# An RWKV-5 attention with a SmeLU feed-forward, rewritten with two tokens per partition and one written order of steps

## The chip, the cores and the metric

One core of one Trainium2 chip. The core has a matrix engine (TensorE, PE), a vector engine (VectorE, DVE), an engine for activation functions (ScalarE, ACT), a general one (GpSimd, POOL), a sequencer for transfers (SyncE, SP) and 16 DMA engines. Each engine works through its own queue in order and waits on semaphores. The metric is device time in microseconds.

## The reference

Four batches, 8 heads, 768 tokens, 48 values per head, all float32. First a linear attention whose state decays by `w` per token and head dimension, with a bonus `u` for the token itself; then two matrix products with a piecewise activation (384 to 2048 to 384).

```python
for t in range(S):
    cur = einsum('bhd,bhe->bhde', u * k[t], v[t])
    y[t] = einsum('bhd,bhde->bhe', r[t], state + cur)
    state = w * state + einsum('bhd,bhe->bhde', k[t], v[t])
x = y as (B * S, H * D)                      # 3072 x 384
h = x @ w_in                                 # 3072 x 2048
g = where(h >= 1, h, where(h <= -1, 0, (h + 1) ** 2 / 4))
out = g @ w_out                              # 3072 x 384
```

## The kernel before

The attention is done in chunks of 128 tokens. A *unit* is one batch of one chunk (128 tokens, all 8 heads); a *group* is two units, batches 0 and 1 or 2 and 3 of the same chunk; there are 12 groups and 24 units. A token lies on a partition, and a head's 48 values are padded to 64, so two heads fill the 128 rows of a matmul.

Per group: R and K are loaded, V too and cast to bf16. `Rs` and `Ks` are R and K times powers of w (tables `Wup` and `Wdn`, made by ScalarE with Ln and Exp; lines 178 to 184). `KU` is K times u, `RKU` is R times KU, its sum over a head is `diag`, and `V2` is V times diag: the bonus term. Per unit: `T` turns Rs and Ks on TensorE (from group 5 on, `TDMA`, a DMA transposes a group's Rs and another its Ks), `A` = Ks by Rs per head (two PSUM banks, four heads each), `AT` = A times the causal mask (two VectorE instructions), `Sp` = Ks by V, the chunk's part of the state, `Tm` adds the old state, `decay` multiplies by w to the 128th (`wCm`), `sbf` casts the state to bf16, `Y` = AT by V plus Rs by the old state, `y` = Y plus V2, and `X` turns y (from group 3 on, `XDMA`, a DMA). Chunk 0 (groups 0 and 1) has no old state.

The feed-forward, per group: four *up* steps q, each 12 matmuls of 256 tokens into a tile `hp` of two PSUM banks (line 471); `relu` and `square` on ScalarE (478, 482); the *gate* on VectorE, min with 1 and max with hp, which writes `gt` (486) and frees hp; then *down* steps, per unit and q four matmuls of 384 columns into one bank `op` (505); a copy and a store per unit.

PSUM: two pairs of banks for hp, and four single banks that T, A, Sp, Y, X and op share. The order is made while the program is built: every operation has an engine, a cost, a key (due time) and needs; a loop at the end of the function (543 to 589) takes, of those ready within a slack, the one with the lowest key. `SHIFT` moves keys by hand. Loads go through SP's queue; R and K of group 1 wait until GpSimd has issued w_in (line 244, a one-element memset that GpSimd does behind it), those of group 2 until the first half of w_out has (line 246, a one-row DMA called `mark`, which SP waits to issue). w_in and w_out go through GpSimd's queue (209, 213). Group 0 is loaded and prepared unit by unit.

Of the kernel before, what the change touches and what calls it, by code (L numbers as in the profile page):

```python
# [1 line left out]

# [15 lines left out]
FG = 4  # L18
UNITS = 2
# [3 lines left out]
def kernel(  # L23
# [13 lines left out]
    NCH = S // C  # L37
# [6 lines left out]
    nQ = nF // FG  # L44
    TOK = UNITS * C
    HID = FG * TOK
    BP = B // UNITS
    nG = NCH * BP

    const = ctx.enter_context(tc.tile_pool(name="const", bufs=1))  # L50
    loads = ctx.enter_context(tc.tile_pool(name="loads", bufs=3))
    pre = ctx.enter_context(tc.tile_pool(name="pre", bufs=2))
    vpool = ctx.enter_context(tc.tile_pool(name="vpool", bufs=5))
    early = ctx.enter_context(tc.tile_pool(name="early", bufs=2))
    att = ctx.enter_context(tc.tile_pool(name="att", bufs=2))
    moe = ctx.enter_context(tc.tile_pool(name="moe", bufs=3))
    gpool = ctx.enter_context(tc.tile_pool(name="gpool", bufs=2 * nQ + 1))
# [17 lines left out]

    w_col = const.tile([P, NP], F32, name="w_col")
    nc.vector.memset(w_col, 1.0)
    zero_col = const.tile([P, 1], F32, name="zero_col")
    nc.vector.memset(zero_col, 0.0)
    one_col = const.tile([P, 1], F32, name="one_col")  # L80
    nc.vector.memset(one_col, 1.0)
    half_col = const.tile([P, 1], F32, name="half_col")
    nc.vector.memset(half_col, 0.5)

# [3 lines left out]
    nc.scalar.dma_start(out=w_bc, in_=bcast(w))  # L88
    nc.scalar.dma_start(out=u_bc, in_=bcast(u))
    i_int = const.tile([P, 1], mybir.dt.int32, name="i_int")  # L90
    nc.gpsimd.iota(i_int, pattern=[[0, 1]], base=0, channel_multiplier=1)
    for j in range(2):
        src = bass.AP(tensor=w.tensor, offset=w.offset + j * D, ap=[[1, D], [2 * D, NP]])
        nc.gpsimd.dma_start(out=w_col[j * HP : j * HP + D, :], in_=src)
    warm = const.tile([P, 1], F32, name="warm")
    nc.scalar.activation(warm, one_col, AF.Ln, bias=zero_col)

# [6 lines left out]

    ident = const.tile([P, P], BF16, name="ident")
    make_identity(nc, ident)
    umask = const.tile([P, P], F32, name="umask")
    nc.gpsimd.memset(umask, 0.0)
    nc.gpsimd.affine_select(
        out=umask, in_=umask, compare_op=ALU.is_ge, fill=1.0,  # L110
        base=0, pattern=[[-1, P]], channel_multiplier=1,
    )

    NB = 3
    Rs = [const.tile([P, UNITS * H, HP], BF16, name="Rs", tag=f"Rs{i}") for i in range(NB)]
    Ks = [const.tile([P, UNITS * H, HP], BF16, name="Ks", tag=f"Ks{i}") for i in range(NB)]
    for i in range(NB):
        nc.vector.memset(Rs[i][:, :, D:], 0.0)
        nc.vector.memset(Ks[i][:, :, D:], 0.0)
    wCm = const.tile([P, NP, 2 * D], F32, name="wCm")  # L120
    nc.vector.memset(wCm, 0.0)
    states = [const.tile([P, NP, 2 * D], F32, name="state", tag=f"st{b}") for b in range(B)]
    states_bf = [const.tile([P, NP, 2 * D], BF16, name="state_bf", tag=f"sb{b}") for b in range(B)]

    lw = const.tile([P, DM], F32, name="lw")
    Wup = const.tile([P, H, D], F32, name="Wup")
    Wdn = const.tile([P, H, D], F32, name="Wdn")
    u_row = u_bc.rearrange("p (h d) -> p h d", h=H)
# [3 lines left out]
    SHIFT = {  # L132
        'Tm': 0.5,
        'V': 2,
        'V2': -2,
        'cast': -2,
        'gate': -0.3,
        'load': 3.3,
        ('Tm', 1): 1.5,
        ('V2', 1): -2,  # L140
        ('att', 1): 3,
        ('gate', 1): 0.7,
        ('load', 3): 3.8,
        ('mm2', 1): -1,
        ('o', 1): -2,
        ('o', 10): 1,
        ('u', 10): 0.5,
        ('w_out', 1): 4,
    }
    FLEX, XDMA, TDMA, VCAST = 3, 3, 5, 12  # L150

    def shift(what, g):
        return SHIFT.get((what, g), SHIFT.get(what, 0.0))


    ops = {}
    users = {}

    def op(name, where, key, fn, needs=(), makes=(), uses=()):
        ops[name] = (where, key, fn, tuple(needs), tuple(makes), tuple(uses))  # L160
        for t in uses:
            users[t] = users.get(t, 0) + 1

    tiles = {}
    engines = {"DVE": nc.vector, "ACT": nc.scalar, "POOL": nc.gpsimd, "SP": nc.sync}

    def psum_bank(shape, dtype, name):
        return lambda i: ps1.tile(shape, dtype, name=name, tag=f"bank{i}")

    def copy(e, out, in_):  # L170
        nc.scalar.copy(out, in_) if e == "ACT" else engines[e].tensor_copy(out, in_)  # L171
# [49 lines left out]
    def turned(n, i, p):  # L221
        g, j = divmod(n, UNITS)
        if g < TDMA:
            return tiles["TT", n][:, i * NP + p, :]
# [395 lines left out]
```

## Time and profile before

| | |
|---|---|
| three runs, us | 189.66, 190.58, 191.42; median 190.58 |
| span of the profiled execution, us | 191.2 |
| DMA: packets, bytes | 103346, 28.11 MB, 97184 of them under 512 B |
| transfers R or K of a group: size, median us from issue to landing | 384 KB, 4.8 and 5.9 |
| each half of w_in: median us from issue to landing | 9.0 |
| ScalarE: relu, square, mean ns | 1114, 1151, 48 of each |
| GpSimd: a product of 128x768, mean ns | 1827 to 1893; 42 of them |

The span reaches from the first to the last instruction of one execution; the page has no other time for that execution. Columns of the table of stretches: start and end, length, busy time of PE, weight loads, DVE, ACT and POOL with their counts of instructions, granted TensorE clock, DMA share, GB/s. A timeline line has start, length, engine, line, operation, output from input, and how often it is repeated; in brackets the idle time before it and what ended it. Lines of groups end with busy time, mean ns, and the idle time before them by its cause. TensorE's durations overlap, since matmuls are pipelined.

### The profile page before, as it was taken

Reading aid. Unit: us, or ns where it says so; the run is one execution under the profiler, and the core shown is the slowest. Engines: PE = TensorE matmul, PEld = TensorE weight load, DVE = VectorE, ACT = ScalarE, POOL = GpSimd, SP = SyncE. Lnnn points to the kernel's source line nnn. Section 1 sums busy time; section 2 is a strip of 40 time slices with the busy share of each in tenths; the row PEclk is TensorE's granted clock in tenths of the full one; section 3 lists DMA queues with packets and bytes.
Section 4 is the critical chain, followed back from the end, with each engine's and each line's share of the span. In section 5 each row is a group of like instructions: output and inputs, shape, how many; then the busy total and the mean of one; then the engine's idle time right before and its main releaser. Section 6 shows DMA issues by size and latency. Waiting matters only on the chain.

```text
span 191.2 us, 4022 instructions
## 1 busy us (share of the span) xinstructions
PE 163.0 (85%) x1602; PEld 118.8 (62%) x1602; DVE 135.6 (71%) x184; ACT 144.9 (76%) x168; POOL 118.0 (62%) x95
## 2 busy tenths in 40 slices
PE   0134676599989899999999998799999999999992
PEld 0023455367867677677677775576777777777760
DVE  3387429954899999897859869678787875754550
ACT  3634369927976699998899979759889877889851
POOL 5293095039599999999998899689898300000000
PEclk9999999969999999999999999999999999999999
DMA  3979989979996389988997698799789421121112
GB/s 93 172 123 186 223 134 159 198 140 221 221 242 122 72 178 202 199 192 191 187 201 153 136 225 167 172 178 207 153 195 137 104 62 24 41 65 41 41 41 82
DMA packets 103346, 28.11 MB, mean 147 GB/s; under 512 B 97184, under 2 KB 102560, under 8 KB 103328
## 3 DMA queue, kind: packets, MB, share of 16 engines
q1 hardware_dynamic: 100096, 24.32, 61.2%
q0 software_dynamic: 2944, 3.15, 11.0%
q10 hardware_dynamic: 288, 0.39, 0.9%
q8 instruction: 12, 0.20, 0.4%
q14 instruction: 6, 0.05, 0.1%
HBM read 20.84 MB, written 4.72 MB: 134 GB/s over the span
## 4 chain that ended last, share of the span: by engine, by line
PE 45%; POOL 26%; DVE 8%; DMA 8%; issue 6%; ACT 4%; SPq 0%; POOLq 0%
PE op L505 22%; PE hp L471 18%; POOL KU L270 6%; POOL Ks L268 5%; POOL RKU L272 5%; POOL V L302 4%; DMA K<-in_k_dram 4%; DMA KT<-Ks 3%; POOL state L406 3%; POOL Rs L266 3%; DVE gt L486 3%; DVE AT L364 2%; PE A L359 2%; DMA xT<-y 1%; DVE Ks L268 1%
## 5 line engine op out<-in xcount | busy, mean ns | idle before, releaser
L486 DVE SCALAR_TENSOR_TENSOR gt<-sq,hp 128x1024 bf16<-128x1024 f32 x48 | 58.5, 1218 | 32.4 <-ACT sq L482 31.9
L471 PE MATMUL hp<-xT,w_in_sb 128*128 128x256 bf16 x576 | 72.8, 279 | 3.8 <-DVE gt L486 1.9
L505 PE MATMUL op<-w_out_sb,gt 128*128 128x384 bf16 x384 | 72.2, 330 | 1.2 <-DVE gt L486 0.7
L478 ACT ACTIVATE pt<-hp,half_col 128x1024 f32<-128x1024 f32 x48 | 53.5, 1114 | 19.6 <-PE hp L471 19.2
L471 PEld LDWEIGHTS <-w_in_sb 128*128 128x128 bf16 x576 | 57.1, 100 | 16.7 <-issue 3.7
L482 ACT ACTIVATE sq<-pt,zero_col 128x1024 f32<-128x1024 f32 x48 | 55.2, 1151 | 1.3
L505 PEld LDWEIGHTS <-gt 128*128 128x128 bf16 x384 | 34.8, 98 | 22.3 <-issue 1.7
L364 DVE TENSOR_TENSOR AT<-A,umask 128x512 bf16<-128x512 f32 x48 | 30.8, 684 | 2.3 <-PE A L359 2.3
L266 POOL TENSOR_TENSOR Rs<-R,Wup 128x768 bf16<-128x768 f32 x11 | 20.1, 1828 | 17.7 <-DMA R<-in_r_dram 17.7
L270 POOL TENSOR_TENSOR KU<-K,u_bc 128x768 f32<-128x768 f32 (+1 forms) x13 | 23.0, 1771 | 4.3 <-DMA K<-in_k_dram 4.2
L272 POOL TENSOR_TENSOR RKU<-R,KU 128x768 f32<-128x768 f32 (+1 forms) x13 | 22.5, 1730 | 0.5
L302 POOL TENSOR_TENSOR V<-V,diag 128x768 f32<-128x768 bf16 x10 | 14.8, 1484 | 6.0 <-ACT V L171 2.2
L406 POOL TENSOR_TENSOR state<-Tm,wCm 128x384 f32<-128x384 f32 x16 | 16.2, 1011 | 3.3 <-DVE Tm L401 3.3
L268 POOL TENSOR_TENSOR Ks<-K,Wdn 128x768 bf16<-128x768 f32 x9 | 16.5, 1833 | 0.0
L393 DVE TENSOR_TENSOR y<-Y,V 128x384 bf16<-128x384 f32 x24 | 13.3, 555 | 2.8 <-POOL Ks L268 1.1
L386 PE MATMUL Y<-V,AT 128*128 128x48 bf16 x192 | 12.0, 188 | 1.9 <-DVE AT L364 1.8
L171 ACT COPY o_sb<-op 128x384 f32<-128x384 f32 x22 | 10.1, 466 | 3.5 <-PE op L505 3.5
L171 ACT CAST state_bf<-state 128x384 bf16<-128x384 f32 x20 | 10.1, 505 | 3.5 <-DVE state L403 2.7
L297 DVE TENSOR_REDUCE diag<-RKU 128x16 f32<-128x768 f32 (+1 forms) x13 | 11.5, 884 | 1.6 <-POOL RKU L272 1.6
L171 ACT CAST V<-VF 128x768 bf16<-128x768 f32 x12 | 9.9, 828 | 3.5 <-DMA VF<-in_v_dram 3.5
L348 PE MATMUL T<-ident,Rs 128*128 128x128 bf16 x40 | 4.3, 237 | 8.8 <-DVE Rs L266 8.5
L386 PEld LDWEIGHTS <-AT 128*128 128x128 bf16 x192 | 10.0, 99 | 2.8 <-DVE AT L364 2.5
(55 smaller groups left out, 109.3 us busy)
## 6 DMA issues: line engine op xcount, KB each, us to landing
VF<-in_v_dram SPq DMA_DIRECT2D x12, 384.0 KB, 4.3
out_dram<-o_sb SPq DMA_DIRECT2D x24, 192.0 KB, 2.4
R<-in_r_dram SPq DMA_DIRECT2D x11, 384.0 KB, 4.8
K<-in_k_dram SPq DMA_DIRECT2D x11, 384.0 KB, 5.9
w_in_sb<-in_moe_w_in_dram POOLq DMA_DIRECT2D x2, 768.0 KB, 9.0
w_out_sb<-in_moe_w_out_dram POOLq DMA_DIRECT2D x2, 768.0 KB, 8.5
R<-in_r_dram SPq DMA_DIRECT2D x2, 192.0 KB, 6.1
K<-in_k_dram SPq DMA_DIRECT2D x2, 192.0 KB, 5.6
```

The costliest lines, as they stand in the source:

```text
L171: nc.scalar.copy(out, in_) if e == "ACT" else engines[e].tensor_copy(out, in_)
L266: engines[e].tensor_mul(part(R_s)[:, :, :, :D], part(R), rep(Wup, j1 - j0))
L268: engines[e].tensor_mul(part(K_s)[:, :, :, :D], part(K), rep(Wdn, j1 - j0))
L270: engines[e].tensor_mul(part(tiles["KU", g]), part(K), rep(u_row, j1 - j0))
L272: engines[e].tensor_mul(part(tiles["RKU", g]), part(R), part(tiles["KU", g]))
L302: engines[e].tensor_mul(tiles["V2", g][:, hs, :], tiles["V", g][:, hs, :], tiles["diag", g][:, hs].unsqueeze(2).to_broadcast([P, n * H, D]),)
L364: nc.vector.tensor_mul(tiles["AT", n][:, i], tiles["A", n][i], umask.unsqueeze(1).to_broadcast([P, NP, P]))
L471: nc.tensor.matmul(hp[:, f, :], w_in_sb[:, i, n0 : n0 + P], tiles["xT", g][:, i, :], start=(i == 0), stop=(i == nK - 1), skip_group_check= ...
L478: nc.scalar.activation(tiles["pt", g, q], tiles["hp", g, q], AF.Relu, bias=half_col, scale=0.5)
L482: nc.scalar.activation(tiles["sq", g, q], tiles.pop(("pt", g, q)), AF.Square, bias=zero_col)
L486: nc.vector.scalar_tensor_tensor(out=gt, in0=tiles.pop(("sq", g, q)), scalar=1.0, in1=tiles.pop(("hp", g, q)), op0=ALU.min, op1=ALU.max)
L505: nc.tensor.matmul(tiles["op", g, j], tiles["gt", g, q][:, f, j * P : (j + 1) * P], w_out_sb[:, n, :], start=(n == 0), stop=(n == nF - 1),)
```

## The change

The whole function is rewritten; what it computes is the same. The order is no longer worked out while building: a string `ORDER` lists every step as `what group.part @engine #slot`, and a loop calls one function per step. Steps and instructions:

- Groups 0 and 1 (`PAIRED`) put two tokens of one unit on a partition, so that 64 partitions hold a unit's 128 tokens and the group's two units lie in the two halves. Loads of these groups have runs of 96 values in place of 48, one DMA per unit. Their tables are for even and odd tokens (`W2`); two of the four are made by Exp, the other two by a product with w on VectorE. Their matmuls work on quarters of the array: A has 64 per group (48 rows by 64, 128 columns), Sp 16, Y 64 (64 rows by 64, 48 columns). Group 0's scaling, bonus, Y and y are split by halves of the heads.
- Two units in one instruction: AT (128x1024) per unit with all heads, y, Tm and decay, casts of the state, xT and the store per group; one DMA transpose for Rs and Ks of a group.
- Four PSUM pairs (`#0` to `#3`) serve all: hp, op, T, A, Sp, Y, X and the fillers.
- `w` is loaded first, on SP; K of group 0 on ScalarE's queue. One table set for Ln and Exp is loaded at the start. The decay column comes from a matmul with ln w (`lc`, `wc`). R, K and V of groups 0 and 1 are issued with no wait; `mk0` makes SP wait for the second half of w_in ahead of group 2's K.
- `kw` issues matmuls of a zero tile, 21, 14, 10, 10 and 3 of them, ahead of steps of TensorE up to `X0`.
- DMA transposes of Rs and Ks from group 3 (before: 5). On VectorE in place of GpSimd: KU of groups 2, 5, 7, 8, RU of 2, Rs of 1 and 3, Ks of 10 and 11, decays of 2 and 7, V2 of 5 and 6; in place of ScalarE the cast of V of 7. On GpSimd in place of VectorE: Ks of groups 1 and 2, V2 of 1. On GpSimd in place of ScalarE: the cast of V of 5, 8, 9, 10 and 11.

```diff
-    psh = ctx.enter_context(tc.tile_pool(name="psh", bufs=2, space=bass.MemoryType.PSUM))
-    ps1 = ctx.enter_context(tc.tile_pool(name="ps1", bufs=1, space=bass.MemoryType.PSUM))
+    psum = ctx.enter_context(tc.tile_pool(name="psum", bufs=1, space=bass.MemoryType.PSUM))
+PAIRED = (0, 1)
+T_BY_DMA, X_BY_DMA = 3, 3
+ORDER = """
+ub ldK0@A tb ln lp wu0 wu1 wd1 kw21#0 lc#0 wd0 vu ldR0 Rs0.0@D KU0.0@P Ks0.0@D KU0.1@P ldK1 kw14#1 T0.0#1 ldR1 Rs0.1@D
+RU0.0@D ldV0 ldV1 Ks0.1@D wi0 us0.0 vd RU0.1@P wc kw10#0 T0.1#2 TT0.0@A TT0.1@A A0.0#3 Rs1@D Ks1@P wi1 Vc0@A Vc1@A
+ud0.0@P kw10#0 A0.1#0 T1.0#1 us0.1 ud0.1@P Sp0#2 AT0.0 Y0.0#3 AT0.1 Y0.1#0 KU1@P wo0 y0.0 y0.1 TT1.0@A Tm0 T1.1#1 mk0
+TT1.1@A kw3#3 X0#3 xT0@D A1.0#0 RU1@P A1.1#2 up0.0#1 re0.0 sq0.0 AT1.0 AT1.1 Sp1#3 us1 ud1@P Tm1 up0.1#0 Y1#2 up0.2#3
+re0.1 sq0.1 ldK2 ga0.0 up0.3#1 re0.2 sq0.2 ldR2 y1 wo1 X1#2 ga0.1 dn0.0.0#0 dn0.0.1 xT1@D up1.0#2 re0.3 ga0.2 up1.1#3
+sq0.3 KU2@D re1.0 dn0.1.0 dn0.1.1 ldK3 RU2@D sq1.0 ga0.3 ga1.0 re1.1 Rs2@P sq1.1 up1.2#1 us2 Ks2@P T2.0#2 TT2.0@D
...
+"""
-    while waiting:
-        found = []
...
-        s, key, _, name, w = min((f for f in found if f[4][0] == w0[0] and f[0] <= s0 + SLACK), key=lambda f: (f[1], f[0]))
...
+    for token in ORDER.split():
+        what, where, e, s = re.fullmatch(r"([A-Za-z]+)([\d.]*)(?:@(\w))?(?:#(\d))?", token).groups()
+        steps[what](e, s, *[int(x) for x in where.split(".") if x])
+    def bank(slot, what, key, shape, dtype):
+        t = psum.tile(shape, dtype, name=what, tag=f"s{slot}")
...
+    def rows(x, g):
+        return x.rearrange("p (h j) d -> p j h d", j=2) if g in PAIRED else x.rearrange("p (j h) d -> p j h d", j=2)
+    def load(queue, tile_, x, g, part):
...
+        if g in PAIRED:
+            for i in range(2):
+                src = x[bp * 2 + i, hs, c * C : (c + 1) * C, :].rearrange("h (q e) d -> q h (e d)", e=2)
+                dst = tile_[i * HP : (i + 1) * HP].rearrange("p (h e) d -> p h (e d)", e=2)[:, hs]
+                queue.dma_start(out=dst, in_=src)
...
+    def step_wu(e, s, i):
+        if i == 0:
+            nc.scalar.activation(flat(W2[0][:, 0]), lw, AF.Exp, scale=up2_col)
+        else:
+            nc.vector.tensor_mul(flat(W2[0][:, 1]), flat(W2[0][:, 0]), w_bc)
+    def step_kw(e, s, n):
+        t = bank(s, "idle", (), [P, P], F32)
+        for _ in range(n):
+            nc.tensor.matmul(t, warm, warm, start=True, stop=True, skip_group_check=True)
-                for p in range(NP):
-                    for i in range(2):
-                        rows = slice(i * HP, i * HP + D)
-                        nc.tensor.matmul(A2[i][:, p, :], turned(n, 1, p)[rows], turned(n, 0, p)[rows], start=True, stop=True)
+    def step_A(e, s, g, h):
...
+            for p in range(NP // 2):
+                for e2 in range(2):
+                    for i in range(2):
+                        ps = slice(i * HP, i * HP + D)
+                        for un in range(2):
+                            q = slice(un * HP, (un + 1) * HP)
+                            nc.tensor.matmul(
+                                A[q, i, p, e2].rearrange("p (e q) -> p e q", e=2), t[ps, 1, e2, 2 * h + p, q], t[ps, 0, :, 2 * h + p, q], start=True, stop=True,
+                                skip_group_check=True,
+                            )
-                nc.vector.tensor_mul(tiles["AT", n][:, i], tiles["A", n][i], umask.unsqueeze(1).to_broadcast([P, NP, P]))
+            mask = mask1.unsqueeze(1).to_broadcast([P, 2 * NP, P])
+            nc.vector.tensor_mul(t.rearrange("p i n t -> p (i n) t"), got("A", g, h).rearrange("p i n t -> p (i n) t"), mask)
+    def step_Y(e, s, g, part=None):
...
+                for i in range(2):
+                    h = 2 * p + i
+                    for f in range(2):
+                        for e2 in range(2):
+                            for un in range(2):
+                                q = slice(un * HP, (un + 1) * HP)
+                                nc.tensor.matmul(
+                                    Y[q, f, (h - h0) * D : (h + 1 - h0) * D], AT[q, i, p % 2, e2, f * HP : (f + 1) * HP], V[q, e2, h, :],
+                                    start=(c == 0 and e2 == 0), stop=(e2 == 1), skip_group_check=True,
+                                )
-                nc.gpsimd.tensor_mul(states[b], tiles.pop(("Tm", n)), wCm)
+    def step_dc(e, s, g):
+        wc = wCm.unsqueeze(1).to_broadcast([P, 2, NP, 2 * D])
+        engines[e].tensor_mul(states[g % BP], got("Tm", g), wc)
+    def step_RK(e, s, g):
+        t = new("RKT", (g,), [P, 2, 2, NP, P], BF16)
+        nc.sync.dma_start_transpose(
+            out=t.rearrange("p x j n t -> p (x j n) t"), in_=RK[g % NB].rearrange("p x j h d -> p (x j h d)")
+        )
+    def step_mk(e, s, i):
+        nc.sync.dma_start(out=mark, in_=(w_in_sb[:1, nK - 1, DF - 16 :],)[i])
```

More of the change, by code (lines that the diff above doesn't have):

```diff
@@ L109 @@
+    mask1 = const.tile([P, P], F32, name="mask1")
+    nc.gpsimd.memset(mask1, 0.0)
     nc.gpsimd.affine_select(
[L110 to L119 removed]
@@ L120 @@
[L120 to L123, printed above, removed]
-    lw = const.tile([P, DM], F32, name="lw")
[L126 to L168, printed above, removed]
@@ new lines, in step_dn, with step_o @@
+    def step_dn(e, s, g, j, q):
+        if j == 0 and q == 0:
+            bank(s, "op", (g,), [P, 2, 512], F32)
+        for f in range(FG):
+            n = q * FG + f
+            nc.tensor.matmul(
+                got("op", g)[:, j, :DO], got("gt", g, q)[:, f, j * P : (j + 1) * P], w_out_sb[:, n, :], start=(n == 0), stop=(n == nF - 1),
+                skip_group_check=True,
+            )
+    def step_o(e, s, g, j):
+        if ("o", g) not in live:
+            new("o", (g,), [P, 2, DO], F32)
+        copy(e, got("o", g)[:, j], got("op", g)[:, j, :DO])
```

686 lines of the change are left out of this document (307 added, 379 removed).

## The prediction

> **What bounds the kernel now.** I read the page first (busy time, then the 40 slices), then the table of stretches, then the chain of waits and TensorE's timeline, and at last VectorE's groups.
>
> ```profile
> span 191.2 us, 4022 instructions
> ...
> PE 163.0 (85%) x1602; PEld 118.8 (62%) x1602; DVE 135.6 (71%) x184; ACT 144.9 (76%) x168; POOL 118.0 (62%) x95
> ...
> PE   0134676599989899999999998799999999999992
> ```
>
> TensorE is the busiest, and its row has two parts: a poor first fifth, then nines to the end. The table of stretches (length, then busy time of each engine) puts numbers to that:
>
> ```profile
> 8.50:22.48 13.98, 6.34 (x62) 4.35 (x63) 10.58 (x15) 5.44 (x9) 7.34 (x14) 1.00 0.97 172
> 22.48:37.86 15.38, 10.89 (x95) 7.88 (x95) 10.01 (x11) 11.59 (x12) 7.22 (x5) 1.00 1.09 167
> 37.86:60.00 22.14, 21.38 (x215) 15.52 (x215) 16.54 (x24) 14.02 (x21) 16.15 (x10) 0.92 1.02 208
> 60.00:90.00 30.00, 29.12 (x330) 21.84 (x327) 27.20 (x37) 26.70 (x31) 30.00 (x21) 1.00 0.76 163
> 90.00:125.00 35.00, 32.86 (x333) 23.94 (x331) 27.79 (x36) 31.00 (x38) 31.59 (x22) 1.00 0.87 176
> ...
> 181.60:191.20 9.60, 5.85 (x36) 3.32 (x34) 2.67 (x3) 3.22 (x4) 0.00 (x0) 1.00 0.17 61
> ```
>
> From 37.86 on TensorE idles 0.76 + 0.88 + 2.14 = 3.8 us until its last matmul ends at 181.60 + 5.85 = 187.45; a tail of 191.2 - 187.45 = 3.75 is left for the last copy and store. Between 22.48, where the first up projection starts, and 37.86 it idles 15.38 - 10.89 = 4.5. So after 22.48 the time is TensorE's work plus its losses. The work, from the chain of waits (start, us) and TensorE's timeline:
>
> ```profile
> 167.24 1.31 PE hp L471 x12
> 168.55 1.30 PE op L505 x8
> ```
>
> ```profile
> 65.33 0.39 PE L348 MATMUL T<-ident,Rs 128*128 128x128 bf16 x4
> ...
> 65.78 0.33 PE L371 MATMUL Sp<-V,Ks 128*128 128x96 bf16 x4
> 65.95 0.21 PE L381 MATMUL Y<-state_bf,TT 128*128 128x96 bf16 x1
> ...
> 66.32 1.47 PE L471 MATMUL hp<-xT,w_in_sb 128*128 128x256 bf16 x12
> 67.73 0.40 PE L359 MATMUL A<-TT 48*128 48x128 bf16 x8
> 68.06 0.82 PE L505 MATMUL op<-w_out_sb,gt 128*128 128x384 bf16 x4
> ```
>
> I take differences of starts, since durations overlap. An up step of 12 matmuls costs 1.31, a down step of 4 costs 0.65. Per unit: eight transposes 65.78 - 65.33 = 0.45, Sp 0.17, Y with the state 66.32 - 65.95 = 0.37, and A 68.06 - (66.32 + 1.31) = 0.43, the switch into it included. Sp gives 42 ns per 96 columns, which leaves 0.37 - 4 x 0.042 = 0.20 for eight 48-column matmuls: 25 ns each.
>
> Work of the kernel before from 22.48: 48 ups 62.9, 96 downs 62.4, 22 A 9.5, 18 Sp 3.1, 20 Y with state and 2 without 7.8, 8 T 3.6, 4 X (three transposes, 0.17 each) 0.7; together 150.0. So 22.48 + 150.0 + 3.75 = 176.2, and 191.2 - 176.2 = 15.0 is lost: idle 4.5 + 3.8, and two stretches at half speed:
>
> ```profile
> 22.48 5.23 PE L471 MATMUL hp<-xT,w_in_sb 128*128 128x256 bf16 x24 [0.57 <-ACT xT L171]
> ```
>
> ```profile
> 38.00:39.00 1.00, 1.00 (x4) 0.44 (x3) 1.00 (x2) 0.26 (x1) 0.00 (x0) 0.50 0.83 162
> 39.00:40.00 1.00, 1.00 (x14) 0.79 (x13) 1.00 (x3) 0.00 (x0) 0.00 (x0) 0.50 0.21 40
> 40.00:41.00 1.00, 1.00 (x4) 0.44 (x3) 1.00 (x3) 0.51 (x1) 0.00 (x0) 0.50 0.61 123
> ```
>
> The first two up steps took 5.23 in place of 2 x 1.31: 2.6 lost (the clock column shows 1.00 there, but the matmuls are twice as long). From about 38 to 41 the granted clock is 0.50: 1.5 lost. That leaves 2.6 that I can't place.
>
> **The change part by part.** *Start.* "w first" and one table set for Ln and Exp:
>
> ```profile
> 5.22 0.62 ACT L178 ACTIVATE lw<-w_bc,zero_col 128x384 f32<-128x384 f32 x1 [1.95 <-DMA w_bc<-in_w_dram]
> 5.85 1.28 ACT L181 ACT_TABLE_LOAD   x1
> 7.15 0.71 ACT L181 ACTIVATE Wup<-lw,zero_col,up_col 128x384 f32<-128x384 f32 x1
> ...
> 7.89 0.56 DVE L266 TENSOR_TENSOR Rs<-R,Wup 128x384 bf16<-128x384 f32 x1 [5.23 <-ACT Wup L181]
> 8.12 1.18 POOL L270 TENSOR_TENSOR KU<-K,u_bc 128x384 f32<-128x384 f32 x1 [4.24 <-DMA K<-in_k_dram]
> 8.48 1.23 DVE L268 TENSOR_TENSOR Ks<-K,Wdn 128x384 bf16<-128x384 f32 x1
> ```
>
> ```profile
> 1.00:2.00 1.00, 0.00 (x0) 0.00 (x0) 0.96 (x8) 0.32 (x1) 0.58 (x1) 1.00 0.00 0
> 2.00:3.00 1.00, 0.00 (x0) 0.00 (x0) 0.63 (x3) 0.99 (x2) 1.00 (x3) 1.00 0.40 136
> ```
>
> The table load of 1.28 goes, but the tables become four, two of them a VectorE product of another (0.56 like the Rs row): 5.22 + 0.62 + 2 x 0.71 + 0.56 = 7.8, no gain. The first products now need all of R and K of group 0, so the four equal transfers ahead of them (w, u, half of R, half of K) become six. The first half of K landed at about 8.0 (KU, which waits for it, starts at 8.12), and data moves from 2 on (last two columns: DMA share, GB/s). Runs are 384 bytes in place of 192: if time goes by the run, R and K cost what their halves did, 8.0; if by the byte, 2 + 6 x 6/4 = 11.0. I take the middle, 9.5. Then VectorE's queue in its new order: five half products (0.56 to 1.23; one at the first, four at the second as they lie beside GpSimd) 5.5; two half sums 1.0; Rs of group 1 (1.09 to 2.40, rows below) 1.7; two joined AT 2.3; a wait for Y of about 1; two half y 1.0; joined state 0.9; xT 0.5; the small ones go by their columns against the half product's 0.56 and the gate's 1.2. Together 13.9, so xT of group 0 at 23.4. TensorE also has A of group 1 ahead of the first up step, and I put that at 24.0, with 21.5 and 26.5 as ends: no earlier than now.
>
> *TensorE's work from there.* Gone are the transposes of groups 3 and 4 (now by DMA, as already from group 5 on) and all of group 1's T and A, done before 24.0. Added: with two tokens per partition, units share a matmul's partitions in halves, so group 1's Sp takes 16 matmuls (0.7) in place of 8 and its Y 64 in place of 16 (64 x 25 ns = 1.6). Sum: 125.3 for ups and downs, T 2 x 0.45 = 0.9, A 20 x 0.43 = 8.6, Sp 0.7 + 16 x 0.17 = 3.4, Y 1.6 + 7.4 = 9.0, X 0.7: 147.9, 2.1 under before. A in quarter tiles (64 per group) has no row; A's eight half-height matmuls of 128 columns start 41 ns apart against 56 for a transpose of the same width, so I bound it by 25 and 56 ns and take 41: 64 x 41 ns = 2.6 per group, ahead of the first up step in both groups. The Trainium skill (TensorEngine Tiling (Array Packing), Key Properties) states that different tiles can load weights and multiply in parallel; four at once would leave 25 ns, the pitch of the shortest matmuls above, so 1.6 per group and the first up step up to 2 us earlier. A's row shows an overlap far short of two at once, so the sum stays with 41.
>
> *Losses.* The gain, if any, is here. Group 1's loads no longer wait for anything, and its T, A and masks are ready before the first up step, so TensorE can go on with Sp, Y and ups of two groups. I laid VectorE's queue beside it: from 23.4 AT 2.3, sums 0.9, state 0.9, first gate (1.2) done at 28.7, y, second gate, xT of group 1 at 31.3, third gate 32.5, KU and RU of group 2 (1.09 to 2.40 each), fourth gate at 36 to 38.5. If it never stops, TensorE comes to where it needs these four gates at 30.2, 31.9, 34.5 and 37.1. So the idle of 4.5 becomes 0 to 1.4; I take 0.5. Half speed: 58 filler matmuls hold TensorE busy before its work; at the slow pitch of transposes (2 x 56 ns) that is 6.5 us in five pieces between waits. What stays lies between 0 and 2.6 + 1.5; I take 1.0, nearer to none. The later idle 3.8 and the unplaced 2.6 I keep.
>
> *VectorE and GpSimd.*
>
> ```profile
> L486 DVE SCALAR_TENSOR_TENSOR gt<-sq,hp 128x1024 bf16<-128x1024 f32 x48 | 58.5, 1218 | 32.4 <-ACT sq L482 31.9
> L364 DVE TENSOR_TENSOR AT<-A,umask 128x512 bf16<-128x512 f32 x48 | 30.8, 684 | 2.3 <-PE A L359 2.3
> ```
>
> ```profile
> 28.71 2.40 DVE L268 TENSOR_TENSOR Ks<-K,Wdn 128x768 bf16<-128x768 f32 x1
> ```
>
> ```profile
> 43.08 1.09 DVE L268 TENSOR_TENSOR Ks<-K,Wdn 128x768 bf16<-128x768 f32 x1 [2.08 <-DMA K<-in_k_dram]
> ```
>
> A 1024-column instruction takes 1.218, two of 512 take 1.368: joining saves 0.15. It is done to 24 AT, 11 y and 10 state updates: 45 x 0.15 = 6.8 us. Against that VectorE takes over eleven full products of two SBUF operands (Rs 1 and 3, Ks 10 and 11, KU 2, 5, 7, 8, RU 2, decays 2 and 7); before it had two. Nine more at 1.09 to 2.40 are 10 to 22 us; V2 and copies, by their columns, some 4 more (an estimate). So VectorE grows from 135.6 to between 143 and 155. It has idle for that: 32.4 us ahead of the gates, nearly all of it waiting for ScalarE. I cost it at nothing on the path; without that cover the extra comes onto TensorE's waits (rival below).
>
> Joined casts, copies and stores shorten ScalarE and SP; its 48 relu and 48 square stay, nothing on the path. The joined DMA transposes of groups 3 and 4 enter SP's queue; SP waits there for Rs and Ks, and the loads behind it wait too. I cost it at nothing, as loads run three buffers ahead; at worst the 2.14 us of idle in 90 to 125, where such transposes serve today, comes once more. A new wait of SP, `mk0` for the second half of w_in, has K and R of groups 2 to 5 behind it; it takes the place of a longer one:
>
> ```profile
> SPq L246 <- DMA w_out_sb<-in_moe_w_out_dram: 9.5, 1, 9.5
> ```
>
> *Sum.* 24.0 + 147.9 + 3.75 + 0.5 + 1.0 + 3.8 + 2.6 = 183.6 against a span of 191.2. The median shown, 190.58, is 0.6 under that span, so 183.0.
>
> **The rivals.**
>
> *Products beside GpSimd (slower).* The Ks product that ran beside GpSimd's KU and RKU took 2.40, the one at 43.08 took 1.09. GpSimd is busy 30.00 of 30.00 in 60:90, so most of the eleven will meet it. Price: 11 x 1.31 = 14.4 us on VectorE, and as much on GpSimd if the wait goes the other way. VectorE's queue is in order; the next gate stands behind the product, and that gate frees one of four PSUM pairs, which hidden, output and attention tiles now share. It decides once a delayed gate is later than TensorE's other ready work, one or two steps, 1.3 to 2.6 us: a single lock of 1.31 is covered, two in a row (KU 2 and RU 2) are not. With all of it on the path 183.0 + 14.4 = 197. Against it: 32 us of VectorE idle. The Trainium skill (SBUF — State Buffer, SBUF: two separate sides) states it as an exclusive lock held for the whole instruction, against an operation with two SBUF inputs. The trace agrees, 2.40 against 1.09. Chance 0.15.
>
> *The start is late.* Loads go by the byte, and w_in, issued behind GpSimd's products, meets 2.4 MB of loads that now run ahead. The first products start at 13.5, past the end of 11.0 above, since w_in and the loads of group 1 share the queues' time, and the first up step comes at 28 in place of 24: 187. For it: the DMA share is 0.97 in 8.50:22.48 already. Against it: runs twice as long. Chance 0.15.
>
> *Nothing is lost.* The order fits so well that of the 7.9 us of losses only 1.5 stay: 176.6. For it: VectorE and ScalarE have idle everywhere. Against it: a fixed order waits wherever one duration is off. Chance 0.13.
>
> **How the numbers follow.** Forecast 0.57, 183.0, its own range 179 to 187 (ends of the start, of half speed and of the joined waits). With the rivals, 8 in 10 lie in 175.5 to 190.5: outside are the upper part of the slower rival and the best of the last. Under 1%, some 1.9 us, a measurement of this kernel (189.66 to 191.42) tells nothing. Faster by more, under 188.7: forecast 0.55, last rival 0.13, two thirds of the late start 0.10: 0.78. Within 1%: 0.08. Slower: 0.14, nearly all from the first rival.
>
> **What would show it.** Right: the first up step between 21.5 and 26; TensorE idle under 2 us in the 15 us behind it; 1.31 and 0.65 per step; the clock at 1.00 around 38. VectorE near 150 us busy with gates still waiting for sq. Wrong: gates preceded by Rs, KU or decay of 2.4 us, TensorE waiting for gt or AT in the middle; products of group 0 starting after 11; A tiles above 56 ns apart.

## The result, and the profile after

The changed kernel takes 206.0 us (median of 4 runs, 205.7 to 206.3) against 190.1 for the kernel before on the same chip: 1.087 times, with a 95% interval of 1.082 to 1.092. 183.0 was forecast. Executions more than 1.5% above the fastest of the same kernel are left out of the comparisons below; where a comparison rests on a single time, the text says so.

The page of the profiled execution of the changed kernel; the 40 slices are 5.1 us each:

```profile
span 203.9 us, 4261 instructions
...
PE 170.5 (84%) x1780; PEld 126.5 (62%) x1780; DVE 153.8 (75%) x155; ACT 126.0 (62%) x142; POOL 104.1 (51%) x76
...
PE   4659279937996999939868699999899999999991
...
PEclk9999759996999999996999999999999999999999
DMA  4999999993099999999999989962704710332004
GB/s 94 210 207 221 169 194 203 165 204 43 7 202 187 151 240 149 238 186 197 152 255 192 228 182 193 216 150 51 141 3 89 219 30 0 102 21 77 3 0 154
```

TensorE's row starts earlier than before and then breaks three times: in slices 5 and 6 (2 and 7), in slices 9 and 10 (3 and 7), and then again and again up to slice 23 (6 in slice 13, 3 in 18, then 8, 6, 8, 6 in 20 to 23), where the kernel before had nines and eights. The transfers stand nearly still in slices 10 and 11, from 45.9 to 56.1 us (43 and 7 GB/s). The table of stretches of the changed kernel puts numbers to the breaks (columns as in the prediction):

```profile
22.50:29.90 7.40, 3.05 (x49) 2.52 (x48) 1.34 (x3) 2.75 (x3) 1.93 (x2) 0.55 1.13 185
29.90:42.50 12.60, 12.60 (x178) 10.28 (x175) 11.92 (x10) 10.41 (x11) 9.52 (x7) 0.99 1.16 184
42.50:50.00 7.50, 2.99 (x17) 2.01 (x16) 6.65 (x5) 1.74 (x3) 1.74 (x1) 0.81 0.77 119
50.00:120.00 70.00, 59.06 (x612) 42.53 (x611) 59.02 (x55) 44.48 (x52) 51.88 (x30) 0.97 1.13 183
120.00:145.00 25.00, 23.90 (x241) 17.36 (x240) 22.73 (x21) 20.24 (x23) 17.43 (x12) 1.00 0.80 142
145.00:199.07 54.07, 53.84 (x492) 39.50 (x492) 36.54 (x35) 38.57 (x41) 8.46 (x5) 1.00 0.27 61
```

Set against the prediction's sum of 183.6: the first up step starts at 29.9 in place of 24.0 (+5.9). Behind it TensorE idles 4.5 + 10.9 + 1.1 + 0.2 and 0.6 at the very end, 17.4 in place of 4.3 (+13.1). Its work with all half speed is 1.7 longer than forecast, the tail 0.35 shorter. Together 203.9. So two terms failed: the start, and the idle that was costed at nearly nothing. Of the 10.9 between 50 and 120, 5.8 end when a transpose made by DMA lands (3.6 for `xT`, 2.2 for `RKT`) and 2.1 with a gate.

**The start.** The timeline of the changed kernel, ScalarE and TensorE:

```profile
17.41 0.83 ACT L117 CAST Vb<-V 128x768 bf16<-128x768 f32 x1
25.00 0.83 ACT L117 CAST Vb<-V 128x768 bf16<-128x768 f32 x1 [6.76 <-DMA V<-in_v_dram]
25.74 1.00 ACT L117 COPY RKT<-T 128x1024 bf16<-128x1024 bf16 x1
...
20.26 1.19 PE L440 MATMUL Y<-Vb,AT 64*64 64x48 bf16 x64
26.80 1.01 PE L329 MATMUL T<-ident,RK 128*128 128x128 bf16 x8 [5.34 <-ACT RKT L117]
...
28.91 1.07 PE L357 MATMUL A<-RKT 48*64 48x128 bf16 x32
29.91 1.56 PE L482 MATMUL hp<-xT,w_in_sb 128*128 128x256 bf16 x12
```

V of group 1 lands at 24.9. Its cast (`Vc1`) stands in ScalarE's queue ahead of the copy `TT1.0`, on which TensorE's next turn waits with X of group 0, and so the first up step, behind it. No step of group 0 needs that cast.

**The idle.** The first piece of it, timeline of VectorE, GpSimd and TensorE in the changed kernel:

```profile
39.18 5.88 DVE L298 TENSOR_TENSOR KU<-K,u_bc 128x768 f32<-128x768 f32 x1
45.09 0.96 DVE L304 TENSOR_TENSOR RU<-R,KU 128x768 f32<-128x768 f32 x1
45.97 2.35 DVE L497 SCALAR_TENSOR_TENSOR gt<-sq,hp 128x1024 bf16<-128x1024 f32 x2
...
38.90 1.81 POOL L298 TENSOR_TENSOR KU<-K,u_bc 128x768 f32<-128x768 f32 x1
40.68 1.80 POOL L289 TENSOR_TENSOR RK<-K,W 128x768 bf16<-128x768 f32 x1
42.45 1.79 POOL L304 TENSOR_TENSOR RU<-R,KU 128x768 f32<-128x768 f32 x1
...
47.24 2.72 PE L482 MATMUL hp<-xT,w_in_sb 128*128 128x256 bf16 x12 [4.51 <-DVE gt L497]
```

One VectorE product lasts 5.88: it begins just behind the first of three GpSimd products that follow each other without a gap, and ends 0.8 behind the last. The two gates behind it come at 46 to 48; TensorE needed the first of them at 42.7, stands 4.5 and then runs a step at half speed. SP stands too (start, length of the issue):

```profile
40.24 3.94 SPq L212 DMA_DIRECT2D R<-in_r_dram  x1
54.68 1.90 SPq L343 DMA_TRANSPOSE RKT<-RK  x1
56.64 1.10 SPq L212 DMA_DIRECT2D K<-in_k_dram  x1
```

From 44.2 to 54.7 SP waits to issue the transpose of group 3, whose `Rs` is also behind VectorE's long product; four loads are queued behind it. That is the hole in slices 10 and 11.

### The profile page after: what moved, and what is told of

Read it like the earlier page. It is cut to its first block, busy times and chain, and to the rows that moved or that the text cites. A ratio compares the mean times of both kernels' runs of the same rounds, so it can differ in the third digit from the quotient of the medians.

```text
span 203.9 us, 4261 instructions
## 1 busy us (share of the span) xinstructions
PE 170.5 (84%) x1780; PEld 126.5 (62%) x1780; DVE 153.8 (75%) x155; ACT 126.0 (62%) x142; POOL 104.1 (51%) x76
## 4 chain that ended last, share of the span: by engine, by line
PE 39%; DMA 27%; DVE 9%; POOL 9%; SPq 5%; issue 5%; ACT 4%; DVEq 0%; POOLq 0%; ACTq 0%
PE hp L482 17%; PE op L504 15%; DMA V<-in_v_dram 9%; DMA RKT<-RK 7%; DMA R<-in_r_dram 6%; DMA K<-in_k_dram 5%; POOL RK L289 4%; DVE gt L497 3%; DVE KU L298 3%; SPq L207 2%; POOL RU L304 2%; PE A L366 2%; POOL V L317 1%; DVE RK L289 1%; SPq L212 1%
## 5 line engine op out<-in xcount | busy, mean ns | idle before, releaser
L489 ACT ACTIVATE pt<-hp 128x1024 f32<-128x1024 f32 x48 | 48.8, 1019 | 39.1 <-PE hp L482 38.9
L493 ACT ACTIVATE sq<-pt 128x1024 f32<-128x1024 f32 x48 | 50.5, 1057 | 5.4 <-DVE gt L497 4.1
L317 POOL TENSOR_TENSOR V<-Vb,us 128x768 f32<-128x768 bf16 (+1 forms) x11 | 14.9, 1364 | 38.7 <-DVE us L310 23.4
L378 DVE TENSOR_TENSOR AT<-A,mask 128x1024 bf16<-128x1024 f32 x20 | 24.1, 1218 | 6.9 <-PE A L366 6.9
L304 POOL TENSOR_TENSOR RU<-R,KU 128x768 f32<-128x768 f32 (+1 forms) x11 | 20.6, 1873 | 0.3
L289 POOL TENSOR_TENSOR RK<-R,W 128x768 bf16<-128x768 f32 x9 | 16.7, 1858 | 6.7 <-DMA R<-in_r_dram 6.7
L289 POOL TENSOR_TENSOR RK<-K,W 128x768 bf16<-128x768 f32 x9 | 17.4, 1932 | 2.8 <-DMA K<-in_k_dram 2.8
L412 POOL TENSOR_TENSOR state<-Tm,wCm 128x768 f32<-128x768 f32 x6 | 10.9, 1821 | 5.0 <-DVE Tm L405 5.0
L460 DVE TENSOR_TENSOR y<-Y,V 128x768 bf16<-128x768 f32 (+1 forms) x13 | 11.5, 888 | 1.7 <-PE Y L440 0.9
L310 DVE TENSOR_REDUCE us<-RU 128x16 f32<-128x768 f32 (+1 forms) x13 | 11.4, 881 | 1.0 <-POOL RU L304 1.0
## 6 DMA issues: line engine op xcount, KB each, us to landing
out_dram<-o SPq DMA_DIRECT2D x6, 192.0 KB, 3.2
R<-in_r_dram SPq DMA_DIRECT2D x4, 192.0 KB, 6.9
```

The lines of the kernel that those rows point to most:

```text
L289: engines[e].tensor_mul(RK[g % NB][:, x, :, hs, :D], rows(got(what, g), g)[:, :, hs], table(x, g, hs))
L304: engines[e].tensor_mul(got("RU", g)[:, :, hs], rows(got("R", g), g)[:, :, hs], got("KU", g)[:, :, hs])
L317: engines[e].tensor_mul(got("V2", g)[:, :, hs], got("Vb", g)[:, :, hs], sums)
L378: nc.vector.tensor_mul(t.rearrange("p i n t -> p (i n) t"), got("A", g, h).rearrange("p i n t -> p (i n) t"), mask)
L489: nc.scalar.activation(t, got("hp", g, q), AF.Relu, bias=0.5, scale=0.5)
L493: nc.scalar.activation(t, got("pt", g, q), AF.Square)
```

## The experiments

Edits are shown in the order's own words: a step with its engine (`@`) and PSUM pair (`#`). "After" is the changed kernel.

### Start and long product, one at a time and together

```diff
# e1, on after
- wi1 Vc0@A Vc1@A ud0.0@P
+ wi1 Vc0@A ud0.0@P
- AT1.0 AT1.1 Sp1#3
+ AT1.0 AT1.1 Vc1@A Sp1#3
# e2, on after
- KU2@D re1.0 dn0.1.0 dn0.1.1 ldK3 RU2@D sq1.0 ga0.3 ga1.0
+ re1.0 dn0.1.0 dn0.1.1 ldK3 sq1.0 ga0.3 ga1.0 KU2@D RU2@D
# e4, on after; e5 is e1 and e4
- KU2@D
+ KU2@P
- RU2@D
+ RU2@P
```

> Theory (a cast in the wrong place): ScalarE's cast of V of group 1 waits for its load until 24.9 and holds the copy that the turning of group 1 and so xT of group 0 wait for; moved behind the first relu and square it frees the start, and the first up step comes at 24 (predicted place) instead of 29.9, the whole 4 to 6 us earlier. Rival (all transfers late anyway): w_in or another load ends last in its place, the first up step stays after 28. Rival (given back): the first up step is early but the middle waits longer for loads, so that the total gains under 2 us.

> Theory (lock with gates behind it): KU of group 2 on VectorE took 5.88 us at 39.2 beside three GpSimd products in a row, and the gates behind it freed the PSUM pairs late. With both gates ahead of KU and RU, TensorE's wait of 4.5 us at 42.7 and the half speed behind it go: 5 to 6 us by 50 us, with KU still far over 1 us long. If the later idle (12 us between 50 and 145) has its own cause, the total gains those 5 to 6; if the late Rs of group 3 causes it, much of the gain is lost or the idle stays. Rival (pairs, not the lock): TensorE still waits over 3 us there.

> Theory (the lock is the root of the middle): with KU and RU of group 2 on GpSimd no VectorE instruction is held there, gates and Rs of group 3 come 4 to 6 us earlier, the empty DMA stretch shrinks, total 6 to 12 us less. Rival (GpSimd has no room): its Rs and Ks of group 2 and products of group 3 come 3.6 us later, attention of group 2 is late, total within 3 us of 206.

> Both edits that helped, the later cast of V of group 1 (4.9 us) and KU and RU of group 2 on GpSimd (6.4 us). If the two losses are separate, they add: 206.0 - 11.3 = 194.7, between 194 and 196, first up step at 23 to 24, no wait over 2 us for a gate before 50. If both only uncover the same later limit (transfers), less than 8 us: above 198.

Single times: e1 201.1, e2 202.1, e4 199.6, beside 191.1 for the kernel before; e3 below, which changes nothing of the two causes, is at 206.0 like the changed kernel. In e4 TensorE has no idle left between 42.5 and 50. In e2 the product behind the gates meets only the last 0.43 of GpSimd's run:

```profile
43.81 1.25 DVE L298 TENSOR_TENSOR KU<-K,u_bc 128x768 f32<-128x768 f32 x1
```

In e1 the first up step starts 6.6 earlier:

```profile
23.31 1.47 PE L482 MATMUL hp<-xT,w_in_sb 128*128 128x256 bf16 x12
...
27.70 0.52 PE L389 MATMUL Sp<-Vb,RK 64*128 64x96 bf16 x16 [2.92 <-ACT Vb L117]
...
39.58 2.60 DVE L304 TENSOR_TENSOR RU<-R,KU 128x768 f32<-128x768 f32 x1 [3.13 <-DMA R<-in_r_dram]
...
43.36 2.72 PE L482 MATMUL hp<-xT,w_in_sb 128*128 128x256 bf16 x12 [4.32 <-DVE gt L497]
```

The second up step is only 3.7 earlier, for `Sp` of group 1 now waits for the same cast. And the second break is there again, with another holder: `RU` of group 2 waits 3.13 for its load and takes 2.60, and the gates stand behind it. What costs is the place ahead of the gates, whether the lock, a late load or both hold the product.

Each cause is real, with 4 to 6.5 us. But together (e5) they give 200.0 (198.7 and 201.3), 1.042 times the kernel before [1.022, 1.061], no better than e4 alone; 194.7 was expected if the two add, over 198 if the same later limit ends both. The table of stretches shows where it went; first e4, then the kernel before:

```profile
42.50:50.00 7.50, 7.50 (x71) 5.46 (x70) 6.54 (x7) 7.08 (x9) 5.53 (x4) 1.00 0.76 132
50.00:120.00 70.00, 59.93 (x606) 43.04 (x605) 59.05 (x54) 44.64 (x52) 54.18 (x31) 0.95 1.21 197
```

```profile
50.00:120.00 70.00, 67.29 (x737) 49.92 (x732) 61.12 (x83) 60.91 (x72) 66.59 (x45) 1.00 0.86 178
```

TensorE idles 10.1 between 50 and 120 in e4, 10.9 in after, 2.7 in the kernel before. In e5 the first up step is 6.6 earlier than in e4, but TensorE then idles 5.9 more ahead of 50 (2.9 of it `Sp` waiting for the cast of V, 3.0 the turn of group 2 waiting for GpSimd's scaled R and K) and 3.1 more between 50 and 120 (13.2). So the gain at the start is given back, most of it before 50.

### What gives it back: transfers, products, turns

```diff
# e3, on after; e9, on e6, with ldK5 ldR5 as well
- RK3 ... ldK4 ... ldV4
+ ldK4 ldV4 RK3
# e6, on e5
- KU5@D KU7@D KU8@D dc2@D dc7@D ud5@D ud6@D Rs3@D Ks10@D Ks11@D Vc7@D
+ KU5@P KU7@P KU8@P dc2@P dc7@P ud5@P ud6@P Rs3@P Ks10@P Ks11@P Vc7@A
# e7, on e5: groups 3 and 4 turned on TensorE
-T_BY_DMA, X_BY_DMA = 3, 3
+T_BY_DMA, X_BY_DMA = 5, 3
- RK3 ... RK4
+ T3.0#1 TT3.0@D ... T3.1#3 TT3.1@A ... T4.0#3 TT4.0@A ... T4.1#0 TT4.1@D
# e8, on e5: one token per partition in groups 0 and 1
-PAIRED = (0, 1)
+PAIRED = ()
# e10, on e6
+            if what == "V32" and g >= 3:
+                live["V32", g] = live["V32", 2]
+                return
```

> Theory (SP's queue): the joined transpose of group 3 stands in SP's queue ahead of K and V of group 4, SP waits there 10 us for Rs of group 3, and the DMA engines stand nearly empty (43 and 7 GB/s in two slices) before a stretch in which they are full to 120. With the two loads ahead of it, the empty stretch shrinks, and TensorE's idle of 12 us from 50 to 145 falls by 3 to 6 us. Rival (the transfers themselves are too many): the middle idle stays within 1.5 us of 12.

> As e5_cast_and_gpsimd, and all other products of two SBUF operands that VectorE took over (KU 5, 7, 8, Rs 3, Ks 10 and 11, decays 2 and 7, V2 5 and 6) back on GpSimd, the cast of V of 7 on ScalarE. Theory (lock in the middle too): VectorE loses some 18 us of work, of which 7 are waiting for GpSimd; TensorE's 10 us of idle from 50 to 145 halve, 3 to 6 us under e5. Rival (GpSimd has no room): its busy time goes to 125 us, attention comes later, no faster than e5 or slower. Rival (transfers are the limit): within 1.5 us of e5.

> As e5_cast_and_gpsimd, with groups 3 and 4 turned on TensorE as before the change (32 transposes more, 1.8 us of TensorE; two joined DMA transposes less). Theory (transposes hold SP's queue and fill the DMA engines): loads of groups 4 and 5 no longer stand behind a wait for Rs of group 3, the slices with little traffic around 45 to 55 fill, the waits for transfers between 60 and 120 shrink, 3 to 6 us under e5. Rival: TensorE's extra work and VectorE's two more copies cost as much, within 1.5 us of e5.

> As e5_cast_and_gpsimd, with groups 0 and 1 like all others, one token per partition (no quarter tiles, runs of 192 bytes, one DMA per load, tables by two Exp). Theory (two tokens per partition bring nothing): a 384-byte packet takes 35.6 ns and two of 192 take 31, so loads land no later, and TensorE has 2 to 3 us less small work: between 2 us faster than e5 and equal. Rival (they shorten the start): first up step over 1.5 us later than in e5, the total too.

> The version with the cast of V of group 1 later and all shared products on GpSimd (198.6 us), and in SP's queue the loads K and V of group 4 and K and R of group 5 moved ahead of the transpose of group 3 that SP waits to issue. Theory 'hole in the transfers': the stretch with almost no transfers (42 to 58 us) closes, R of group 5 is issued near 46 in place of 53, the TensorE idle between 50 and 120 falls by 5 us or more, and the time comes to 190 to 194. Theory 'the transfers as a whole are too many from there on': the hole only moves, the time stays within 1.5 us of 198.6. Theory 'in-order waits on the engines': the same, within 1.5 us of 198.6, though loads land earlier.

> The same version (198.6 us) with the nine loads of V of groups 3 to 11 left out: those groups take the V of group 2, so their outputs are others; every engine has the same instructions. It takes away 9 of the 36 loads of R, K and V. Theory 'transfers are the limit behind the start': TensorE's idle between 50 and 120 goes and the time comes to 185 to 190. Theory 'in-order waits on the engines, whatever the loads do': 195 or more.

| | e3 | e5 | e6 | e7 | e8 | e9 | e10 |
|---|---|---|---|---|---|---|---|
| time, us | 206.0 | 200.0 | 198.6 | 198.8 | 201.2 | 198.7 | 193.4 |
| first up step | 30.0 | 23.4 | 23.0 | 24.0 | 28.4 | 24.5 | 24.4 |
| TensorE idle 50 to 120 | 10.7 | 13.2 | 12.7 | 11.3 | 12.2 | 12.6 | 7.5 |

e3 and e10 are single times. Idle is 70 less TensorE's busy time in the stretch. e3 and e9 answer to the hole: the loads go out earlier, but the time stays. In e9 the transposes that SP now issues behind them slip from 45.8 to 53.4, and TensorE waits 8.6 for what they bring; so e9 moves the hole's cost rather than taking it away, and what the hole alone costs is not shown. e6 and e7 each undo one move and gain a little over 1 us, within the spread of e5; the theories behind e3, e6, e7 and e9 asked for 3 us or more. e8 starts 5 us later and its time is 1.2 above e5's, within the spread of the two (199.8 and 202.5): a late start is made good in the middle as an early one is given back, and that two tokens per partition bring nothing fails for the start. e7 takes 1.9 of the idle away; e10, with nine loads of 384 KB fewer, takes 5.2: the transfers are part of it, but 7.5 us stay, and its 193.4 lies between its two theories.

In e10's timeline the longest wait of that stretch is no transfer's: TensorE waits for a state update on VectorE, and VectorE, just ahead of it, for a GpSimd product:

```profile
102.78 0.40 PE L369 MATMUL A<-RKT 48*128 48x128 bf16 x8 [2.20 <-DVE Tm L408]
...
100.91 0.95 DVE L313 TENSOR_REDUCE us<-RU 128x16 f32<-128x768 f32 x1 [3.40 <-POOL RU L307]
101.78 0.95 DVE L408 TENSOR_TENSOR Tm<-Sp,state 128x768 f32<-128x768 f32 x1
```

### The two moves alone, in the kernel before

```diff
# b1
-    FLEX, XDMA, TDMA, VCAST = 3, 3, 5, 12
+    FLEX, XDMA, TDMA, VCAST = 3, 3, 3, 12
# b2: Rs of 3, KU of 5, 7, 8, Ks of 10, 11
+                if (g, i) in ((3, 0), (5, 2), (7, 2), (8, 2), (10, 1), (11, 1)):
+                    where = (("DVE", 1.1),)
```

> The kernel before with one part of the change: groups 3 and 4 are turned by DMA too (two transposes per group more in SP's queue, 16 transposes less on TensorE), the planner works the rest round it. As the prediction had it (nothing on the path, 0.9 us of TensorE work less): 189 to 191. Theory 'transposes in SP's queue hold the loads back': 192 to 196.

> The kernel before with one part of the change: Rs of group 3, KU of 5, 7 and 8 and Ks of 10 and 11 on VectorE in place of GpSimd; the planner works the rest round it. As the prediction had it (covered by VectorE's idle): 189.5 to 192. Rival 'products beside GpSimd': six locks of 1.3 us or more come through to TensorE, 195 to 199.

b1 takes 1.019 times the kernel before [1.012, 1.025], 3.6 us of 192.0; b2 1.029 times [1.021, 1.037], 5.5 us. The prediction had both at nothing. The planner arranges everything anew around each, so the prices hold for the move together with what the planner makes of it. The one Rs that b2 moves, and TensorE's up steps in b2:

```profile
L266 DVE TENSOR_TENSOR Rs<-R,Wup 128x768 bf16<-128x768 f32 x1 | 2.3, 2325 | 0.0
...
L473 PE MATMUL hp<-xT,w_in_sb 128*128 128x256 bf16 x260 | 32.0, 272 | 6.6 <-DVE gt L488 4.9 <-DMA xT<-y 1.7
```

From 50 on the kernel before has 1.3 of idle ahead of its up steps, nearly all for xT and none for gates: the 4.9 us of waits for gates are new. Two of the five, 0.73 and 1.84, come behind a moved product that took 2.3 and 2.1 on VectorE, as the slower rival had it. The other three do not: three of the six moved products took only 0.95 to 1.05, and b1, which moves no product, has 4.2 of waits for gates as well (traced in its longest execution, 198.1). So the price of the move is shown, and the rival's chain for about half of these waits.

### Both moves undone, and what is left

```diff
# e11, on e6: the edit of e7
# e12, on e11: loads moved as in e9
# e13, on e11
- Vc8@P ldV9 ldV10 Y6#2 y6 ldK9 RU8@P ... ga5.0 RK7
+ Vc8@P RK7 ldV9 ldV10 Y6#2 y6 ldK9 RU8@P ... ga5.0
# e14, on e13
+ up0.1#0 Sp1#3, dn1.1.2 T3.0#1, dn1.1.3 T3.1#3, dn2.0.0#1 dn2.1.0 T4.0#3
# e15, on e13; e16 the same on e14
- Vc5@P Vc8@P Vc9@P Vc10@P Vc11@P
+ Vc5@A Vc8@A Vc9@A Vc10@A Vc11@A
- KU8@P Rs8@P Ks8@P ... RU7@P
+ RU7@P KU8@P Rs8@P Ks8@P
```

> Cast of V of group 1 later, all shared products on GpSimd (198.6 us so far) and now also groups 3 and 4 turned on TensorE again. Each of the two moves alone cost the kernel before 3.6 and 5.5 us. Theory 'the two moves are the loss in the middle': TensorE's wait of 5.1 us for the turned group goes, SP is never held with loads behind it, and the time comes to 192 to 194.5. Theory 'GpSimd is the limit once the products are back on it': 197 or more, with GpSimd without idle between 50 and 120.

> The same with the loads K and V of group 4 and K and R of group 5 moved ahead of ScalarE's square of group 1's last step in SP's queue, which nothing of the turning now stands behind. Theory 'hole in the transfers between 42 and 58': the hole closes for good, group 5 is ready sooner and another 1.5 to 3 us go, 189.5 to 192. Theory 'the hole costs nothing once the turning is on TensorE': within 1 us of the version without it.

> Both moves undone (195.75 us) and one step of SP's queue moved: the DMA transpose of group 7 ahead of the loads V of 9 and 10 and K of 9 in place of behind them. The trace of that version has TensorE waiting 3.66 us for this transpose at 101.8, while its inputs were ready at 95.0 and SP issued it at 99.9; the two up steps behind the wait ran at half speed, 2.74 us for 12 matmuls. Theory 'SP's order behind a full queue of transfers': 4 to 5 us less, 191 to 192.5. Rival 'GpSimd, busy without a break from 60 to 110, sets the pace': the wait moves to the next step that GpSimd feeds, within 1.5 us of 195.75.

> The same, and five steps of TensorE moved ahead of steps that wait: the second up step of group 0 ahead of group 1's Sp (wait 2.92 us), two down steps of group 1 ahead of group 3's turns (0.54 and 1.05 us), two of group 2 ahead of group 4's turn (1.49 us). If the waits in TensorE's order are what is left, 3 to 4 us less than the version before it, 187 to 189, which is under the kernel before. If something else sets the pace: within 1 us of it.

> The version with both moves undone and the transpose of group 7 earlier (195.5 us), with work taken from GpSimd and put in another order there: the casts of V of 5, 8, 9, 10 and 11 on ScalarE as in the kernel before (0.83 us each on GpSimd), and R times KU of group 7 ahead of three products for group 8. In the trace TensorE's wait at 102 (2.24 us, half speed behind it) goes back through VectorE's state update and its sum of group 7 to that product, which ended at 102.1. Theory 'GpSimd's queue sets the pace': the wait goes and the time falls by 2.5 to 4 us, 191.5 to 193. Rival 'one wait only makes room for the next': within 1 us of 195.5.

> The same with the five steps of TensorE moved ahead as in the run on fills. Its one undisturbed time was 194.6; by the first theory 190.5 to 192, about the kernel before; by the rival 194 or more.

e11 takes 195.75, 1.024 times the kernel before [1.017, 1.030]: with the two moves and the two causes of the first 50 us undone, 6.3 of the 8.7 percent are gone. 192 to 194.5 was expected, so the theory holds for its direction and falls short by 1 to 4 us. Its table of stretches:

```profile
50.00:120.00 70.00, 62.23 (x665) 46.22 (x664) 50.25 (x49) 48.15 (x55) 64.76 (x40) 0.95 1.03 184
```

TensorE still idles 7.8 here. GpSimd is busy 64.8 of 70, but in the kernel before it is busy 66.6 while TensorE idles 2.7: a full GpSimd by itself is not the reason. e12 gave 193.6 to 200.1, and the two times that count, 193.6 and 195.6, are 1.018 [1.006, 1.030]: whether the loads help is not settled. The rest, wait by wait: e11's longest wait of TensorE in that stretch, then what stands in the same place in e13, then e15's longest:

```profile
105.44 0.61 PE L366 MATMUL A<-RKT 48*128 48x128 bf16 x8 [3.66 <-DMA RKT<-RK]
105.98 2.74 PE L482 MATMUL hp<-xT,w_in_sb 128*128 128x256 bf16 x12
```

```profile
104.36 0.61 PE L366 MATMUL A<-RKT 48*128 48x128 bf16 x8 [2.24 <-DVE Tm L405]
105.22 2.62 PE L482 MATMUL hp<-xT,w_in_sb 128*128 128x256 bf16 x12 [0.25 <-DVE y L460]
```

```profile
112.94 2.74 PE L482 MATMUL hp<-xT,w_in_sb 128*128 128x256 bf16 x12 [5.14 <-DMA xT<-y]
```

Each mended wait left room for another near it: the turn of group 7, then the state update behind VectorE's sum and GpSimd's product, then the turn of y of group 6, which SP issues at 110.2 behind the transpose of group 8, though y had been written by 101.2. The times: e13 195.5, 1.014 [1.007, 1.022]; e14 194.6 once, its three other executions 199.3 to 200.8; e15 195.9 to 197.9, 1.036 [1.005, 1.067], with two times of the kernel before beside it; e16 195.6 and 196.6, 1.027 [0.995, 1.060], unclear. The 2.5 to 5 us that e13, e14 and e15 were to bring did not come: the rivals that one wait only makes room for the next were nearer. No version is under the kernel before. What would have to be rearranged at once was not found, and the last 1.4 to 2.4 percent, 3 to 4.5 us, stay open.

## Why the prediction was wrong

- **Right:** TensorE idles 0 between 29.9 and 42.5 behind its first up step, as laid out; an AT of 1024 columns takes 1.218, so joining saves what was forecast; VectorE is busy 153.8 (143 to 155); the tail is 3.4.
- **The first step that failed: the start.** The working followed TensorE's and VectorE's queues to 24.0 and left out ScalarE's: the cast of V of group 1 ahead of `TT1.0`, for a load that lands at 24.9. Moved, it gives a first up step at 23.3 (e1), within the forecast's ends. The rival of a late start had its size nearly right (28) and its reason in part: that load is issued by 12.8, among the loads that now run ahead, and lands at 24.9. But the first products were not late (GpSimd's start at 8.5, VectorE's at 10.4, not at 13.5), and the rival had no cast in it.
- **The step that cost most: "I cost it at nothing on the path"**, for the products on VectorE, and again for the transposes in SP's queue. A sum of VectorE's idle was taken as cover. In the trace a single product took 5.88 and came just ahead of two gates that TensorE needed from 42.7 on, 3.5 us behind its start. The slower rival named this chain, and `KU` and `RU` of group 2 as the pair that would not be covered, but put a lock at 1.31, one GpSimd instruction, and held a single one covered; here `KU` alone took 5.88 and `RU` behind it 0.96. With both on GpSimd (e4) 4.5 us of idle go. SP's wait "at worst 2.14" was 10.4 in one piece. In the kernel before the two moves cost 5.5 and 3.6.
- **Also off:** the later idle, 3.8, was carried over unchanged from an order that the change does away with; it became 12.3 (10.9, 1.1 and 0.2). Two terms were too high and did not hurt: A has 32 quarter tiles per group, not the 64 of the working and of the section on the change, and they take 0.85 at full clock (e1), not 2.6; Y of group 1 takes 1.13, not 1.6. `mk0` holds SP for 11.6, so it takes the place of a 9.5 that was shorter, not longer. Half speed was not cured by the fillers: the clock column has 0.55 ahead of the first up step and 0.81 behind the next break. TensorE had stood 5.34 and 4.51 there; where e1 and e4 take these waits away, the column has 1.00 and an up step takes 1.47.
- **Settled and not:** the late cast, the product beside GpSimd and the two moves are shown, and with all four undone 1.087 becomes 1.024. Their prices do not add, since each is partly given back later. What is left between 50 and 120 is waits in turn on SP, VectorE and GpSimd; that the written order as a whole is the cause is argued, not shown. The four shared PSUM pairs, the joining of two units and `mk0` were not varied.

## What to carry to other kernels

Follow every engine's queue to the first critical step, the one with little work too: a step that waits for a late load holds back whatever is behind it. A product given to VectorE beside a run of GpSimd products can last as long as the whole run (5.88 here), and one whose load is late holds its queue as well (3.13 in e1); its price is then what stands right behind it, and VectorE's idle over the whole kernel does not cover it. And where several queues are nearly full, a gain at the start shows in the end time only if the middle can go on at TensorE's pace: look for the idle of every stretch, not for the mended wait.

## What the runs showed of the hardware

- A VectorE product with two SBUF operands took 0.94 to 0.96 alone, 5.88 beside three GpSimd products in a row, which themselves kept to 1.8. The Trainium skill (SBUF — State Buffer, SBUF: two separate sides) has the lock held for a whole instruction; in this run it was not handed over between instructions that follow each other without a gap. It is not always so: in e1 `RU` (39.58 to 42.18) ended 0.8 behind the first of two GpSimd products in a row, and the second of these took 2.52 in place of 1.8.
- Quarter tiles do run side by side, as the Trainium skill (TensorEngine Tiling (Array Packing), Key Properties) has it for different tiles: in the changed kernel the step behind the 64 matmuls of Y of group 1 starts 1.13 us after they do, 17.6 ns each, against the 25 that the prediction works out for the same width; A's 32 take 0.85 at full clock (e1), 27 ns each, against 41 for its half-height form.
- One packet of 384 bytes took 35.6 ns in the changed kernel, where two of 192 took 38.8; in the kernel before two of 192 took 31.0. So the longer runs, from two tokens per partition, saved little per byte. Without them (e8) SP takes 7.4 to issue V of groups 0 and 1 (e5: 3.9), and the first up step is 5 us later than in e5; but e8 also changes the number of transfers and of tables, and no run parts these. Mean time of a packet, from the records of all 16 engines:

```
              192 B             384 B            256 B
before        15.5 ns x 73728   -                22.5 ns x 21248
after         19.4 ns x 61440   35.6 ns x 6144   26.8 ns x 25344
```

- `relu` and `square` take 95 ns less each in the changed kernel, 9 us of ScalarE in all; it gives them the bias as a constant in place of a tile, and no run here parts that from the rest. The Trainium skill (ScalarE: Activation LUTs, What ACT_TABLE_LOAD costs) states that a bias or scale read per partition adds some 93 ns to an instruction; the trace agrees, 1114 to 1019 and 1151 to 1057:

```profile
L489 ACT ACTIVATE pt<-hp 128x1024 f32<-128x1024 f32 x48 | 48.8, 1019 | 39.1 <-PE hp L482 38.9
...
L493 ACT ACTIVATE sq<-pt 128x1024 f32<-128x1024 f32 x48 | 50.5, 1057 | 5.4 <-DVE gt L497 4.1
```
